# A decayed attention feeding two gated layers on one core: the first pair's sums in two pieces and k's transposes one step earlier

## The chip, the cores and the metric

The kernel runs on one core of one Trainium2 chip. The metric is the device time of one execution, in microseconds (us). The kernel before takes 1025.54 us, the median of three runs (1025.13 to 1026.08). Engines are named as in the profile: PE is TensorE (PEld its weight loads), DVE is VectorE, ACT is ScalarE, POOL is GpSimd, SP is SyncE, which issues the DMAs.

## The reference

Inputs are q, k and v of shape (4, 8, 576, 64), that is 4 batches of 8 heads, and f of shape (4, 8, 576), all in float32. First comes causal attention with a decay, then two layers of products:

```python
scores = (1 / sqrt(64)) * q @ k.T
cum    = cumsum(log(clip(f, 1e-4, 1.0)), axis=-1)
decay  = cum[:, :, :, None] - cum[:, :, None, :]
scores = where(causal, -1e9, scores + decay)
scores = scores - max(scores)
attn   = exp(scores); attn = attn / (sum(attn) + 1e-9)
x      = (attn @ v).transpose(0, 2, 1, 3).reshape(2304, 512)

xn  = x / sqrt(mean(x * x) + 1e-6) * rms_g
g   = xn @ w_gate;  silu = g / (1 + exp(-g))
y   = (silu * (xn @ w_val)) @ w_out          # 512 -> 1536 -> 512
h   = y @ w_in                               # 512 -> 2048
out = (h / (1 + exp(-h))) @ w_out2           # 2048 -> 512
```

## The kernel before, in words

**Attention.** The 32 heads are worked through as 16 pairs, two heads side by side on the 128 partitions. A pair's 576 queries are cut into nine blocks of 64; one block of both heads against its keys is a unit. A unit with block number c has (c+1)*64 keys; the units of a pair run in the order of `ORDER`, that is with 64, 128, 512, 192, 448, 256, 384, 320 and 576 columns. For one unit PE makes the scores in three products (L472: q and k each stand as a high and a low part, and high*high, high*low and low*high are added in one PSUM bank). DVE adds the decay and takes the maximum in one instruction (L475, followed by a short read of the accumulator, tile `nm`). ACT takes the exponential (L488). Four steps later (`TURN`) PE transposes the result in pieces of 128 columns (L497; the 576-column unit has four of these and one more at L504), and DVE or ACT copies them out of PSUM (L278, L280, tiles `g` and `gl`). Six steps later (`USE`) a whole pair is multiplied with v (L528). POOL forms the decay (L459) and the mask on its diagonal (L461) one step ahead of the scores.

**Operands of the next pair.** While a pair runs, k and q of the next are loaded (L396, L398) and transposed by PE (`operand`, L425, tiles `nk` and `nq`, four transposes of 128 columns each; the last 64 rows of both at L442). ACT writes the rounded high part (L273) and DVE the rest (L274), for k as one 128x512 piece each, for q as two halves of 64 partitions. The operands of odd and even pairs lie in the tiles `op0h`, `op0l` and `op1h`, `op1l`. The steps at which this happens are counted from the start of the pair in the table `WHEN`: k at -6, q at -5.

**PSUM.** The scores, and the transposes of k and q, take turns in four banks (tiles called `s`); what is transposed after the exponential, and the first part of the product with v, uses three others (tiles called `t`). A new user of a bank waits until the last reader of the old one is done.

**The start.** `warm` (L247 to L250) multiplies zeros to keep PE busy: 12 products ahead of everything, then 1, 2 and 5 more at three later places (`WARM`). Meanwhile f is clipped (L567, DVE), its logarithm taken (L568, ACT), summed along the row (L570, DVE), scaled (L571, DVE) and negated (L575, ACT); c is transposed (L581) and copied (L584), and for the first pair the negated sums are spread over the partitions by two products with a 0/1 matrix (L411) and copied to `ncb` (L412). The other pairs read them back from DRAM (L419).

**Behind attention.** The weights of the layers are loaded and decoded while attention runs (`weights`, L143 to L154; conversions to high and low parts at L192, L193 and L205, L206). From about 200 us on the kernel consists of PE's products for the layers.

**What sets the order.** The program is written as a loop over steps (L643 on) that runs one unit's part after another, with the rest hung on step numbers by `at` (L630); a scheduler then sorts each engine's instructions, in its own estimate of when they are ready, except where `issue_after` or `later` holds one back. Each engine runs its instructions in that order, one after the other.

Of the kernel before, what the change touches and what calls it, by code (L numbers as in the profile page):

```python
# [30 lines left out]
WARM = (12, 1, 2, 5)  # L31
# [31 lines left out]
def block_kernel(ctx: ExitStack, tc: tile.TileContext, q, k, v, f, w_gate, w_val, w_o1, rms_g, w_in, w_o2, ident_d, sel_d, hot_d, out):  # L63
# [66 lines left out]

    def weights(w, src, cols, key):
# [12 lines left out]
        dst = stp.tile([P, 2 * n], I32, tag="st", name="st")  # L144
        pr = dst.rearrange("p (n t) -> p n t", t=2)
        nc.sync.dma_start(out=dst if cols is None else dst.rearrange("p (c f) -> p c f", f=cols), in_=src)
# [67 lines left out]
    def attention():  # L214
        exps, maxima = [], []
        with ExitStack() as st:
# [30 lines left out]
            def warm(n):  # L247
                ps = bank(pst)
                for _ in range(n):
                    nc.tensor.matmul(ps[:, :384], lhsT=ops[1][0][:, :P], rhs=ops[1][0][:, :384], start=True, stop=True)  # L250
# [21 lines left out]
            def split(hi, lo, src):  # L272
                nc.scalar.activation(out=hi, in_=src, func=AF.Copy)  # L273
                nc.vector.tensor_tensor(out=lo, in0=src, in1=hi.bitcast(F32), op=ALU.subtract)  # L274
# [107 lines left out]
            class Pair:  # L382
# [20 lines left out]
                def load_sums(self, between=None):  # L403
# [4 lines left out]
                    if h == 0:  # L408
                        for w in (slice(0, HS), slice(HS, S)):
                            bp = bank(pss)[:, : w.stop - w.start]  # L410
                            nc.tensor.matmul(bp, lhsT=hot, rhs=n8[:, w], start=True, stop=True)  # L411
                            told = nc.scalar.activation(out=t[:, w], in_=bp, func=AF.Copy)  # L412
                            if w.start == 0:
                                with tc.issue_after(told.ins):
                                    between()
                    else:
                        with tc.issue_after(self.held):
                            for j in range(2):
                                nc.sync.dma_start(out=t[j * D : (j + 1) * D], in_=nc8d[h + j, :].partition_broadcast(D))  # L419

                def operand(self, nm, lone=False):
# [4 lines left out]
                    if nm == "k":  # L426
                        split(self.oh[:, QW + D :], self.ol[:, QW + D :], ps)
                    else:
# [5 lines left out]

                        half(0)
                        if lone:
                            return _p(half, 1)
                        half(1)

                def operand_tails(self):  # L440
                    tl = bank(pss)
                    self.turned = nc.tensor.transpose(tl[:, :P], self.n["q"][:, FULL].rearrange("p j d -> p (j d)"), ident).ins  # L442
                    for j in range(2):
                        js, w = slice(j * D, (j + 1) * D), P - j * D
                        at_ = slice(QW - w, QW + w)
                        hi, lo = (o[js, at_].rearrange("p (i w) -> p i w", w=w)[:, :, :D] for o in (self.oh, self.ol))
                        split(hi, lo, tl[js, :P].rearrange("p (i w) -> p i w", w=D))

            class Rows:
# [13 lines left out]
                def scores(self):  # L463
# [19 lines left out]
                    if c % 2 == 0 and c < BLOCKS - 1:  # L483
                        nc.gpsimd.memset(self.pr[:, n : n + D], 0.0)
# [73 lines left out]
            nc.sync.dma_start(out=hot, in_=hot_d)  # L558
# [18 lines left out]
            with tc.issue_after(pairs[0].turned):  # L577
                warm(WARM[1])
            cps = bank(pss)
            for c in range(BLOCKS):  # L580
                nc.tensor.transpose(cps[:D, c * BH : (c + 1) * BH], c8[:, c * D : (c + 1) * D], ident[:BH, :BH])  # L581
            cj = cps[:D, : BLOCKS * BH].rearrange("p (c n j) -> p c n j", c=BLOCKS, j=2)
            for j in range(2):
                nc.vector.tensor_copy(c8t[j * D : (j + 1) * D], cj[:, :, :, j])  # L584
            second = pairs[0].operand("q", lone=True)
            with tc.issue_after(pairs[0].turned):
                warm(WARM[2])
            pairs[0].load_sums(second)
            pairs[0].operand_tails()
            with tc.issue_after(pairs[0].turned):  # L590
# [446 lines left out]
```

## Time and profile before

| | before |
|---|---|
| median of 3 runs | 1025.54 us (1025.13 to 1026.08) |
| the profiled execution | 1025.31 us |
| its span, first to last instruction | 1023.5 us |
| granted TensorE clock, mean | 1.000 |
| PE busy | 1011.4 us |
| DVE, ACT, POOL busy | 761.1, 566.9, 401.2 us |

The rows further down come from a page that sums up one profiled execution, and from views of its trace. A row of the timeline has the start in us, the duration in us, the engine, the line of the kernel, the operation, its output and inputs with their shapes, and a count; rows that follow each other on one engine with the same line and shape are drawn into one. In square brackets stands how long the engine was idle before it and what ended that. Matmuls are pipelined: the time from one start to the next is what a row of them costs, and the duration shown is longer than that. The same is true to a smaller degree for DVE and ACT: the next instruction often starts 0.05 to 0.1 us before the one ahead ends.

### The profile page before, as it was taken

Reading aid. Unit: us, or ns where it says so; the run is one execution under the profiler, and the core shown is the slowest. Engines: PE = TensorE matmul, PEld = TensorE weight load, DVE = VectorE, ACT = ScalarE, POOL = GpSimd, SP = SyncE. Lnnn points to the kernel's source line nnn. Section 1 sums busy time; section 2 is a strip of 40 time slices with the busy share of each in tenths; the row PEclk is TensorE's granted clock in tenths of the full one; section 3 lists DMA queues with packets and bytes.
Section 4 is the critical chain, followed back from the end, with each engine's and each line's share of the span. In section 5 each row is a group of like instructions: output and inputs, shape, how many; then the busy total and the mean of one; then the engine's idle time right before and its main releaser. Section 6 shows DMA issues by size and latency. Waiting matters only on the chain.

```text
span 1023.5 us, 16104 instructions
## 1 busy us (share of the span) xinstructions
PE 1011.4 (99%) x5463; PEld 847.7 (83%) x5463; DVE 761.1 (74%) x1520; ACT 566.9 (55%) x1193; POOL 401.2 (39%) x613
## 2 busy tenths in 40 slices
PE   9999999999999999999999999999999999999998
PEld 7787788878888888888888888888888888888887
DVE  7889887877778797976688768846666696466664
ACT  7998989873444232544544556564444464534441
POOL 8777666511022026331365334435533322222310
PEclk9999999999999999999999999999999999999999
DMA  5764533123544444231334122223322233121102
GB/s 140 193 189 114 126 92 94 27 63 124 185 142 167 159 150 154 73 124 49 106 124 143 64 65 79 83 83 114 113 83 83 83 124 144 42 71 54 52 1 83
DMA packets 114162, 106.40 MB, mean 104 GB/s; under 512 B 62896, under 2 KB 83792, under 8 KB 114080
## 3 DMA queue, kind: packets, MB, share of 16 engines
q1 hardware_dynamic: 112352, 102.23, 32.5%
q10 hardware_dynamic: 1728, 3.15, 1.0%
q8 instruction: 43, 0.70, 0.3%
q14 instruction: 39, 0.32, 0.1%
HBM read 79.59 MB, written 25.76 MB: 103 GB/s over the span
## 4 chain that ended last, share of the span: by engine, by line
PE 77%; DVE 2%; issue 0%; ACT 0%
PE t L778 40%; PE s L778 20%; PE x L778 16%; PE o L528 0%; DVE hl L696 0%; PE s L303 0%; DVE b11l L696 0%; DVE c L912 0%; PE t L497 0%; PE t L528 0%; DVE f L151 0%; DVE ms L342 0%; ACT pr L488 0%; DVE c L152 0%; DVE wl L174 0%
## 5 line engine op out<-in xcount | busy, mean ns | idle before, releaser
L206 POOL TENSOR_TENSOR wol<-c,woh 128x512 fp32r<-128x512 f32 x53 | 78.7, 1491 | 241.8 <-ACT woh L205 218.3
L696 DVE TENSOR_TENSOR hl<-c,hh 128x512 fp32r<-128x512 f32 (+1 forms) x140 | 114.4, 825 | 45.3 <-ACT hh L695 44.4
L167 POOL TENSOR_TENSOR f<-f 128x256 f32<-128x256 f32 x112 | 93.7, 859 | 112.9 <-DMA f<-keptb 51.2
L695 ACT ACTIVATE hh<-c 128x512 fp32r<-128x512 f32 (+1 forms) x140 | 79.7, 582 | 46.3 <-DVE c L912 41.6
L790 ACT ACTIVATE c<-t 128x512 f32<-128x512 f32 x84 | 49.8, 593 | 95.0 <-PE t L778 93.9
L459 POOL TENSOR_SCALAR dt<-ncb,c8t 128x64 f32<-128x64 f32 (+2 forms) x144 | 79.2, 552 | 35.9 <-DVE nm L475 27.5
L488 ACT ACTIVATE pr<-pr,nm 128x192 f32<-128x192 f32 (+3 forms) x144 | 80.2, 558 | 11.6 <-DVE nm L475 8.1
L905 ACT ACTIVATE c<-c 128x512 f32<-128x512 f32 x66 | 41.6, 630 | 80.8 <-DVE c L795 80.8
L475 DVE CUSTOM_DVE_ANT_0 pr<-s,dt 128x256 f32<-128x256 f32 (+7 forms) x160 | 70.1, 450 | 13.4 <-PE t L497 4.8
L193 POOL TENSOR_TENSOR wl<-f,wh 128x1024 fp32r<-128x1024 f32 x12 | 28.8, 2396 | 125.6 <-ACT wh L192 118.9
L497 PE MATMUL t<-ident,pr 128*128 128x128 f32 x384 | 69.2, 279 | 3.7 <-ACT pr L488 2.6
L174 DVE TENSOR_TENSOR wl<-f,wh 128x1024 fp32r<-128x1024 f32 (+1 forms) x48 | 57.7, 1209 | 20.4 <-ACT wh L172 20.2
L795 DVE TENSOR_TENSOR c<-t,c 128x512 f32<-128x512 f32 x60 | 41.1, 687 | 39.4 <-ACT c L790 26.2
L172 ACT ACTIVATE wh<-f 128x1024 fp32r<-128x1024 f32 (+1 forms) x56 | 54.4, 973 | 23.4 <-PE x L778 18.9
L778 PE MATMUL s<-hh,woh 128*128 128x512 f32 (+1 forms) x172 | 64.0, 372 | 0.2 <-DVE xa L959 0.2
L778 PE MATMUL s<-hh,wol 128*128 128x512 f32 (+1 forms) x172 | 64.0, 372 | 0.0
L778 PE MATMUL s<-hl,woh 128*128 128x512 f32 (+1 forms) x172 | 63.9, 372 | 0.0
L977 DVE TENSOR_TENSOR xa<-x,xa 128x512 f32<-128x512 f32 x64 | 43.5, 682 | 25.2 <-PE x L778 25.1
L977 DVE TENSOR_TENSOR xa<-s,xa 128x512 f32<-128x512 f32 (+1 forms) x63 | 42.9, 683 | 25.5 <-PE s L778 25.1
L905 ACT ACTIVATE c<-t 128x512 f32<-128x512 f32 (+1 forms) x74 | 37.9, 512 | 35.9 <-PE t L778 33.8
L148 ACT ACTIVATE f<-st 128x512 f32<-128x512 f32 x42 | 27.8, 668 | 53.6 <-DMA keptb<-f 18.1
L959 DVE TENSOR_TENSOR xa<-s,xa 128x512 f32<-128x512 f32 (+1 forms) x72 | 45.4, 638 | 14.0 <-PE s L778 13.9
(248 smaller groups left out, 3234.1 us busy)
## 6 DMA issues: line engine op xcount, KB each, us to landing
st<-in_moe_w_out_dram SPq DMA_DIRECT2D x28, 512.0 KB, 3.7
st<-in_moe_w_in_dram SPq DMA_DIRECT2D x16, 512.0 KB, 3.8
f<-keptb SPq DMA_DIRECT2D x32, 256.0 KB, 2.6
st<-in_moe_w_gate_dram SPq DMA_DIRECT2D x12, 512.0 KB, 4.2
kepta<-f SPq DMA_DIRECT2D x24, 256.0 KB, 2.3
st<-in_moe_w_val_dram SPq DMA_DIRECT2D x12, 512.0 KB, 4.6
f<-kepta SPq DMA_DIRECT2D x24, 256.0 KB, 2.8
out_dram<-xa SPq DMA_DIRECT2D x17, 256.0 KB, 2.0
```

The costliest lines, as they stand in the source:

```text
L167: nc.gpsimd.tensor_tensor(out=out_, in0=x, in1=y, op=op)
L174: (nc.gpsimd if plain and i else nc.vector).tensor_tensor(out=lo[i][:, v], in0=f[i][:, v], in1=hi[i][:, v].bitcast(F32), op=ALU.subtract)
L206: nc.gpsimd.tensor_tensor(out=lo, in0=f, in1=hi.bitcast(F32), op=ALU.subtract)
L459: nc.gpsimd.tensor_scalar(out=dt, in0=p.nct[:, 0 if last else D :][:, :n], scalar1=c8t[:, c, p.i : p.i + 1], scalar2=1.0, op0=ALU.add, op1 ...
L475: reduced = nc.vector.tensor_tensor_reduce(out=self.pr[:, ks], in0=sp, in1=self.dt[:, ks], op0=ALU.add, op1=ALU.min, scale=-SCALE, scalar= ...
L488: e = nc.scalar.activation(out=pr, in_=pr, func=AF.Exp, bias=self.nm, scale=-1.0, accum_out=p.batch.sums[:, self.c, p.hp : p.hp + 1])
L497: nc.tensor.transpose(pt[:, jj * P : (jj + 1) * P], keys[:, jj * P : (jj + 1) * P], ident)
L695: nc.scalar.activation(out=hi, in_=src, func=AF.Copy)
L696: nc.vector.tensor_tensor(out=lo, in0=src, in1=hi.bitcast(F32), op=ALU.subtract)
L778: nc.tensor.matmul(ps, lhsT=l, rhs=r, start=start and z == 0, stop=stop and z == len(mms) - 1, skip_group_check=not (start and stop))
L905: act = nc.scalar.activation(out=hf, in_=a, func=AF.Silu)
L977: nc.vector.tensor_tensor(out=a, in0=ps, in1=a, op=ALU.add)
```

## The change

Three things are changed.

- **k's transposes.** From the third pair on (`n > 1`) the step of k in `WHEN` is one smaller, so that PE transposes k of the next pair in front of the four transposes of the 576-column unit (L537 in the new numbering), and no longer behind the scores of the 192-column unit. ACT's and DVE's split of k follows it.
- **The start.** `WARM` goes from (12, 1, 2, 5) to (12, 2, 2, 4). The clip, the logarithm and the sum are each cut in two pieces of 256 and 320 columns. The scaling instruction goes; its factor is put into the two instructions behind (`scale=-ISC` where the sums are negated, a multiplication where c is copied). The negated sums come ahead of k's split on ACT; q is transposed ahead of c; the products that spread the sums come behind the last transpose of q's and k's tails, and both are now issued together.
- **Loads.** The first two loads of w_gate are tied to the load of q of pair 4 (`FETCH`), the 0/1 matrix is loaded ahead of q's tails, and the decay of the first pair's 576-column unit waits for the last clearing of padding on the same engine.

```diff
-WARM = (12, 1, 2, 5)
+WARM = (12, 2, 2, 4)
+HEAD = 256
+FETCH = 4
...
                     for nm in "kq":
-                        at(s + WHEN[nm], _p(p.operand, nm))
+                        at(s + WHEN[nm] - (nm == "k" and n > 1), _p(p.operand, nm))
...
+                        if nm == "q" and not self.i:
+                            nc.sync.dma_start(out=hot, in_=hot_d)
+                        if nm == "q" and self.i == FETCH:
+                            for m in range(2):
+                                fetch_in(w_gate, "a0", m)
...
+                def first_sums(self, w):
+                    if w.start == 0:
+                        self.nct = dec.tile([P, S], F32, tag="ncb", name="ncb", bufs=2)
+                    bp = bank(pss)[:, : w.stop - w.start]
+                    self.spread = nc.tensor.matmul(bp, lhsT=hot, rhs=n8[:, w], start=True, stop=True).ins
+                    def copy():
+                        return nc.scalar.activation(out=self.nct[:, w], in_=bp, func=AF.Copy).ins
+                    return copy
...
-            nc.vector.tensor_scalar(out=lf, in0=ft, scalar1=1e-4, scalar2=1.0, op0=ALU.max, op1=ALU.min)
-            nc.scalar.activation(out=lf, in_=lf, func=AF.Ln)
+            cols = (slice(0, HEAD), slice(HEAD, S))
+            for w in cols:
+                nc.vector.tensor_scalar(out=lf[:, w], in0=ft[:, w], scalar1=1e-4, scalar2=1.0, op0=ALU.max, op1=ALU.min)
+            for w in cols:
+                nc.scalar.activation(out=lf[:, w], in_=lf[:, w], func=AF.Ln)
             table = nc.scalar.activation(out=first, in_=lf[:, :1], func=AF.Exp)
-            nc.vector.tensor_tensor_scan(out=c8, data0=on, data1=lf, initial=0.0, op0=ALU.mult, op1=ALU.add)
-            scaled = nc.vector.tensor_scalar(out=c8, in0=c8, scalar1=ISC, scalar2=None, op0=ALU.mult)
-            with tc.issue_after(table.ins), tc.issue_after(scaled.ins):
-                pairs[0].operand("k")
-            for to, of in ((slice(D, S), slice(0, SF)), (slice(0, D), slice(SF, S))):
-                nc.scalar.activation(out=n8[:, to], in_=c8[:, of], func=AF.Copy, scale=-1.0)
+            for w in cols:
+                before = 0.0 if w.start == 0 else c8[:, HEAD - 1 : HEAD]
+                nc.vector.tensor_tensor_scan(out=c8[:, w], data0=on[:, w], data1=lf[:, w], initial=before, op0=ALU.mult, op1=ALU.add)
+            one = pairs[0]
+            k_parts = one.operand("k", lone=True)
+            with tc.issue_after(one.turned):
+                warmed = warm(WARM[1])
+            with tc.issue_after(warmed):
+                q_parts = one.operand("q", lone=True)
+            with tc.issue_after(table.ins):
+                for to, of in ((slice(D, S), slice(0, SF)), (slice(0, D), slice(SF, S))):
+                    negated = nc.scalar.activation(out=n8[:, to], in_=c8[:, of], func=AF.Copy, scale=-ISC)
...
+            with tc.issue_after(negated.ins):
+                k_high, k_low = k_parts()
...
+            with tc.issue_after(warmed):
+                near, far = (one.first_sums(w) for w in (slice(0, HS), slice(HS, S)))
+            near()
+            far()
+            tails()
+            with tc.issue_after(one.spread):
                 warm(WARM[3])
```

Below is PE's order of before where the sixth pair hands over to the seventh, at 70 to 74 us of the trace; the rows from the 576-column unit's transposes to the scores of the 256-column unit (`op1h` belongs to the pair that runs, `nk` and `nq` are k and q of the next).

```order
L310 MATMUL s<-ident,ss 64x98
L497 MATMUL t<-ident,pr 128x128 x4
L504 MATMUL t<-ident,pr 64x128
L472 MATMUL s<-op1h 128x192
L472 MATMUL s<-op1l,op1h 128x192
L472 MATMUL s<-op1h,op1l 128x192
L425 MATMUL s<-ident,nk 128x128 x4
L497 MATMUL t<-ident,pr 128x128
L472 MATMUL s<-op1h 128x448
```

After the change the same place of PE reads:

```order
L325 MATMUL s<-ident,ss 64x98
L448 MATMUL s<-ident,nk 128x128 x4
L537 MATMUL t<-ident,pr 128x128 x4
L544 MATMUL t<-ident,pr 64x128
L512 MATMUL s<-op1h 128x192
L512 MATMUL s<-op1l,op1h 128x192
L512 MATMUL s<-op1h,op1l 128x192
L537 MATMUL t<-ident,pr 128x128
L512 MATMUL s<-op1h 128x448
```

The four transposes of k went from behind the 192-column scores to ahead of the 576-column unit's transposes; the rest kept its order.

On ACT the same place of before reads as follows (`op0h` 128x512 is k's high part for the next pair, `pr,sums` the exponentials, `wh` a weight's high part):

```order
L488 ACTIVATE pr,sums<-pr,nm 128x128
L192 ACTIVATE wh<-f 128x1024
L488 ACTIVATE pr,sums<-pr,nm 128x512
L278 ACTIVATE gl_145<-t 64x128
L488 ACTIVATE pr,sums<-pr,nm 128x192
L273 ACTIVATE op0h<-s 128x512
```

and after the change:

```order
L528 ACTIVATE pr,sums<-pr,nm 128x128
L205 ACTIVATE wh<-f 128x1024
L528 ACTIVATE pr,sums<-pr,nm 128x512
L287 ACTIVATE op0h<-s 128x512
L293 ACTIVATE gl_145<-t 64x128
L528 ACTIVATE pr,sums<-pr,nm 128x192
```

k's high part moved ahead of two instructions, and still stands behind the weight's conversion and the exponential of 512 columns.

On DVE, again at this place, before (`g` 128x4x128 is the copy of the 576-column unit's transposes, the instructions called ISA are those with the maximum, now L515):

```order
L280 COPY g_1225<-t 128x4x128
L475 ISA pr,nm<-s,dt 128x192
L475 ISA nm 128x1
L280 COPY g_1398<-t 128x128
L475 ISA pr,nm<-s,dt 128x448
L475 ISA nm 128x1
L274 TENSOR_TENSOR op0l<-s,op0h 128x512
```

and after the change:

```order
L295 COPY g_1231<-t 128x4x128
L288 TENSOR_TENSOR op0l<-s,op0h 128x512
L515 ISA pr,nm<-s,dt 128x192
L515 ISA nm 128x1
L295 COPY g_1404<-t 128x128
L515 ISA pr,nm<-s,dt 128x448
L515 ISA nm 128x1
```

k's low part moved from behind the 448-column unit to ahead of the 192-column unit.

## Rows read from the trace of the kernel before

**Rows 1.** The page: busy time, share of the span and instructions of each engine.

```profile
PE 1011.4 (99%) x5463; PEld 847.7 (83%) x5463; DVE 761.1 (74%) x1520; ACT 566.9 (55%) x1193; POOL 401.2 (39%) x613
```

**Rows 2.** Stretches: from:to, us, then busy us of each engine, PEclk, DMA share, GB/s.

```profile
12.00:187.00 175.00, 169.05 (x1347) 141.08 (x1345) 146.17 (x532) 160.69 (x472) 124.29 (x324) 1.00 0.52 134
...
200.00:1000.00 800.00, 798.86 (x3870) 670.15 (x3870) 582.95 (x905) 382.67 (x666) 259.60 (x240) 1.00 0.30 99
```

**Rows 3.** Waits of PE: tile and line, what ended them: us, times, longest.

```profile
PE t L497 <- ACT pr L488: 2.6, 8, 0.5
...
PE s L371 <- DVE nm L475: 1.0, 1, 1.0
```

**Rows 4.** Timeline at 110 to 113 us, PE and DVE.

```profile
110.03 0.66 PE L497 MATMUL t<-ident,pr 128*128 128x128 f32 x4 [0.45 <-ACT pr L488]
...
111.27 0.69 DVE L280 COPY g<-t 128x512 f32<-128x512 f32 x1
...
111.87 0.35 DVE L475 CUSTOM_DVE_ANT_0 pr<-s,dt 128x192 f32<-128x192 f32 x1
...
112.57 0.36 PE L472 MATMUL s<-op0h 128*128 128x256 f32 x1
```

**Rows 5.** Timeline at 71 to 75 us, PE.

```profile
71.31 0.60 PE L425 MATMUL s<-ident,nk 128*128 128x128 f32 x4
...
71.75 0.27 PE L497 MATMUL t<-ident,pr 128*128 128x128 f32 x1
...
72.46 0.60 PE L425 MATMUL s<-ident,nq 128*128 128x128 f32 x4
...
73.77 0.39 PE L472 MATMUL s<-op1h 128*128 128x256 f32 x1
```

**Rows 6.** Timeline at 71 to 75 us, ACT and DVE.

```profile
71.22 1.05 ACT L192 ACTIVATE wh<-f 128x1024 fp32r<-128x1024 f32 x1
...
72.17 0.72 ACT L488 ACTIVATE pr<-pr,nm 128x512 f32<-128x512 f32 x1
...
72.88 0.26 ACT L278 ACTIVATE gl<-t 64x128 f32<-64x128 f32 x1
...
74.09 0.69 DVE L274 TENSOR_TENSOR op0l<-s,op0h 128x512 fp32r<-128x512 f32 x1 [0.67 <-ACT op0h L273]
```

**Rows 7.** Timeline of ACT at 112, 118, 124 and 175 us.

```profile
112.77 0.58 ACT L273 ACTIVATE op1h<-s 128x512 fp32r<-128x512 f32 x1
...
118.53 0.63 ACT L205 ACTIVATE woh<-f 128x512 fp32r<-128x512 f32 x1
...
124.36 0.73 ACT L488 ACTIVATE pr<-pr,nm 128x512 f32<-128x512 f32 x1
...
174.89 0.72 ACT L488 ACTIVATE pr<-pr,nm 128x512 f32<-128x512 f32 x1
```

**Rows 8.** Timeline of PE at 126 and 177 us.

```profile
126.03 0.65 PE L528 MATMUL t<-g,vn 128*64 128x256 f32 x2
126.61 0.39 PE L472 MATMUL s<-op1h 128*128 128x256 f32 x1
...
177.46 0.39 PE L472 MATMUL s<-op1h 128*128 128x256 f32 x1
```

**Rows 9.** Timeline at 151 to 153 us, DVE and PE.

```profile
151.80 0.35 DVE L475 CUSTOM_DVE_ANT_0 pr<-s,dt 128x192 f32<-128x192 f32 x1
...
152.21 0.39 PE L472 MATMUL s<-op1h 128*128 128x256 f32 x1
```

**Rows 10.** Timeline of the start.

```profile
1.32 4.21 PE L250 MATMUL t<-op1h 128*128 128x384 f32 x12 [1.32 <-DVE op1h L245]
...
6.26 0.46 DVE L571 TENSOR_SCALAR c<-c 32x576 f32<-32x576 f32 x1
...
6.89 0.76 ACT L575 ACTIVATE n<-c 32x512 f32<-32x512 f32 x2
...
9.37 1.12 PE L250 MATMUL t<-op1h 128*128 128x384 f32 x5
```

More of the change, by code (lines that the diff above doesn't have):

```diff
@@ L129, in words, with fetch, fetch_in @@
         return (w, 1) if w.dtype == F32 else (w.bitcast(I32), 2)
+    fetched = {}
+    def fetch(src, cols):
+        dst = stp.tile([P, 2 * DM], I32, tag="st", name="st")
+        nc.sync.dma_start(out=dst if cols is None else dst.rearrange("p (c f) -> p c f", f=cols), in_=src)
+        return dst
+    def fetch_in(w, key, m):
+        w, s = words(w)
+        if s > 1:
+            fetched[key, m] = fetch(w[:, s * m * P : s * (m + 1) * P].rearrange("(c p) f -> p c f", p=P), s * P)
     def weights(w, src, cols, key):
@@ L214, in attention @@
     def attention():
-        exps, maxima = [], []
+        exps, maxima, padded = [], [], []
         with ExitStack() as st:
@@ L272, in split @@
             def split(hi, lo, src):
-                nc.scalar.activation(out=hi, in_=src, func=AF.Copy)
-                nc.vector.tensor_tensor(out=lo, in0=src, in1=hi.bitcast(F32), op=ALU.subtract)
+                high = nc.scalar.activation(out=hi, in_=src, func=AF.Copy)
+                low = nc.vector.tensor_tensor(out=lo, in0=src, in1=hi.bitcast(F32), op=ALU.subtract)
+                return high, low
             def move(which, out, in_):
@@ L407, in load_sums @@
                     h = b * H + 2 * hp
[L408 to L419, printed above, removed]
+                    with tc.issue_after(self.held):
+                        for j in range(2):
+                            nc.sync.dma_start(out=t[j * D : (j + 1) * D], in_=nc8d[h + j, :].partition_broadcast(D))
                 def operand(self, nm, lone=False):
@@ L426, in operand @@
                     if nm == "k":
-                        split(self.oh[:, QW + D :], self.ol[:, QW + D :], ps)
+                        whole = _p(split, self.oh[:, QW + D :], self.ol[:, QW + D :], ps)
+                        if lone:
+                            return whole
+                        whole()
                     else:
@@ L433, in half, with halves, operand_tails, both @@
                             split(hi, lo, ps[js].rearrange("p (c w) -> p c w", w=D))
+                        def halves():
+                            parts = [[o[j * D : (j + 1) * D, : FULL * 2 * P].rearrange("p (c j w) -> p c j w", j=2, w=D)[:, :, j] for o in (self.oh, self.ol)] for j in range(2)]
+                            of = [ps[j * D : (j + 1) * D].rearrange("p (c w) -> p c w", w=D) for j in range(2)]
+                            for (hi, lo), src in zip(parts, of):
+                                nc.scalar.activation(out=hi, in_=src, func=AF.Copy)
+                            for (hi, lo), src in zip(parts, of):
+                                nc.vector.tensor_tensor(out=lo, in0=src, in1=hi.bitcast(F32), op=ALU.subtract)
+                        if lone:
+                            return halves
                         half(0)
-                        if lone:
-                            return _p(half, 1)
                         half(1)
-                def operand_tails(self):
+                def operand_tails(self, lone=False):
                     tl = bank(pss)
                     self.turned = nc.tensor.transpose(tl[:, :P], self.n["q"][:, FULL].rearrange("p j d -> p (j d)"), ident).ins
[L443 to L447, printed above, removed]
+                    def both():
+                        for j in range(2):
+                            js, w = slice(j * D, (j + 1) * D), P - j * D
+                            at_ = slice(QW - w, QW + w)
+                            hi, lo = (o[js, at_].rearrange("p (i w) -> p i w", w=w)[:, :, :D] for o in (self.oh, self.ol))
+                            split(hi, lo, tl[js, :P].rearrange("p (i w) -> p i w", w=D))
+                    if lone:
+                        return both
+                    both()
             class Rows:
@@ L576, in attention @@
+            with tc.issue_after(table.ins):
+                for to, of in ((slice(D, S), slice(0, SF)), (slice(0, D), slice(SF, S))):
+                    negated = nc.scalar.activation(out=n8[:, to], in_=c8[:, of], func=AF.Copy, scale=-ISC)
             nc.sync.dma_start(out=nc8d, in_=n8)
[L577 to L578 removed]
+            with tc.issue_after(negated.ins):
+                k_high, k_low = k_parts()
             cps = bank(pss)
[L580 to L581 removed]
+            with tc.issue_after(one.turned):
+                for c in range(BLOCKS):
+                    turned = nc.tensor.transpose(cps[:D, c * BH : (c + 1) * BH], c8[:, c * D : (c + 1) * D], ident[:BH, :BH])
@@ L582, in attention @@
             cj = cps[:D, : BLOCKS * BH].rearrange("p (c n j) -> p c n j", c=BLOCKS, j=2)
[L583 to L590, printed above, removed]
+            with tc.issue_after(k_low.ins):
+                for j in range(2):
+                    scaled = nc.vector.tensor_scalar(out=c8t[j * D : (j + 1) * D], in0=cj[:, :, :, j], scalar1=ISC, scalar2=None, op0=ALU.mult)
@@ new lines, in attention @@
+            with tc.issue_after(k_high.ins), tc.issue_after(scaled.ins):
+                q_parts()
+            with tc.issue_after(turned.ins):
+                tails = one.operand_tails(lone=True)
+            with tc.issue_after(one.turned):
+                warmed = warm(WARM[2])
+            with tc.issue_after(warmed):
[4 more added lines that the diff above has]
+            with tc.issue_after(one.spread):
```

14 lines of the change are left out of this document (7 added, 7 removed).

## The prediction

> **What bounds the kernel now.** I read the busy times first: PE is at work for 1011.4 of 1023.5 us, the next engine, DVE, for 761.1 [rows 1]. Then the stretches. From 200 to 1000 us PE is busy for 798.86 of 800 us, so nothing can be won there, and what attention gives up or wins before goes straight to the end. In attention, 12 to 187 us, PE is busy for 169.05 of 175 us, ACT for 160.69, DVE for 146.17 [rows 2]. So PE has some 6 us of idle time there, and ACT, at 92%, has hardly more than twice that: whatever is put ahead of an exponential on ACT pushes work that PE waits for. Third the waits of PE: the largest group is the one in front of the 576-column unit's transposes, which wait for ACT's exponential, 2.6 us in eight waits of at most 0.5 us; the longest single wait is 1.0 us, at the sums of squares [rows 3]. Seven of the eight stand where one pair hands over to the next. Last I followed the hand-overs in the timeline one by one, and set beside each the order that the changed program has there and what each instruction there waits for.
>
> **k's transposes moved.** Fourteen hand-overs are changed, at 22, 33, 45, 57, 71, 84, 98, 110, 124, 137, 149, 162, 175 and 188 us. PE's four transposes of k take 0.44 us from their start to the next instruction's [rows 5]. Put ahead of the 576-column transposes, they fill the wait, which is at most 0.45 us (110.03 in [rows 4]). But the transposes lie in one of four banks, and the bank is handed on only when DVE has made k's low part. By the bank order of the changed program the bank's next user is, at most hand-overs, the 256-column unit with its scores, and at three of them the transposes of q. What counts is when k's split is done.
>
> - At 22, 33 and 45 us the split is done before its bank is wanted. The waits that go there are 0 at 22 us, 0.14 and 0.16 us at the others: -0.30.
> - At 57, 110 and 162 us the 0.45 us wait goes, but the 256-column scores now wait for k's low part, which stands behind the copy of 512 columns. At 110: that copy starts at 111.27 and the next instruction 0.60 later, at 111.87 [rows 4]; the split takes 0.68 to 112.55, and the scores start some 0.06 later at 112.61, against 112.57 before [rows 4]. So +0.04 each, +0.12 together: the gain is eaten up.
> - At 84, 137 and 188 us the 256-column scores waited for the maximum of the 192-column unit and still do: 0.
> - At 98 and 149 us there was no wait to be won, and k's split now stands between the copy and the maximum of the 192-column unit. At 149 the copy is done at 151.80, when the 192-column maximum started [rows 9]; the split ends 0.69 later [rows 6], at 152.49, and the scores start at 152.55 against 152.21 [rows 9]: +0.34. At 98 worked in the same way +0.32. Together +0.66.
> - At 71, 124 and 175 us an earlier tile of the sums of squares shifts the turn of the banks, and it is q's transposes that take k's bank. PE then stands still from the end of the 448-column scores until k is split, and the split is late, since its high part on ACT stands behind the exponential of 512 columns, which is itself behind a weight's conversion. At 71: the exponential starts at 72.17 and what follows it at 72.88 [rows 6]; k's high part takes 0.58 [rows 7] to 73.46, the low part 0.71 with its start (0.69 in [rows 6]) to 74.17, q's transposes start near 74.20 (72.46 before) and take 0.44, so that the 256-column scores start at 74.64 and not at 73.77 [rows 5]: +0.87. At 124 the conversion of a weight that stood at 118.53 [rows 7] moves behind and in front of this exponential: 0.55 us (its 0.63 less the overlap). So 124.36 [rows 7] becomes 124.91; 0.71, 0.58 and 0.71 more are 126.91, and with 0.06 and 0.44 the scores start at 127.41 against 126.61 [rows 8]: +0.80; one of the two products with v that stood ahead of them now stands behind, at 0.29 (126.03 to 126.61 for two [rows 8]): +1.09. At 175 the exponential is earlier against PE: 174.89 [rows 7] and the same 2.00 are 176.89, the scores start at 177.39 against 177.46 [rows 8], -0.07, and with the 0.29 it is +0.22. Together +2.18.
>
> Behind these points PE's later work hangs on the same banks and on DVE's maxima, which move along, so I let the delays stand in full.
>
> **The start.** The scaling of 0.46 us [rows 10] goes from the path, and cutting clip, logarithm and sum in two allows some overlap. Against this, the negated sums (two instructions, 0.76 [rows 10]) now stand ahead of k's high part on ACT and no longer behind it, and the product that spreads the first piece of the sums gets the bank of k's transposes: it waits for k's low part now, which only the second piece did before. The bounds are the whole scaling won (-0.46) and the whole of the negation lost (+0.76). I take their sum, +0.30, since both lie on the one path from the sums to the spread; what the overlap of pieces gives is taken back by POOL, whose decays follow each other without a gap behind it. The warming products stay 20 in number.
>
> **The loads.** w_gate's first two loads were issued between the loads of k and q of pair 4 and are now behind q's, some 4 us later; they feed a conversion on DVE and ACT that nothing in attention waits for. Zero; if the cover fails, it costs POOL or ACT time inside the waits already counted.
>
> **The sum.** -0.30 + 0.12 + 0 + 0.66 + 2.18 + 0.30 = +2.96 us. The profiled execution took 1025.31 us, 0.23 under the median, so it stands for the others; on the median this gives 1028.5 us. What the unknown terms allow: the start from -0.46 to +0.76, and the waits at 71, 124 and 175 from 0.5 (if the conversions on ACT come a place later) to 3.0 (if the delay of the 192- and 448-column maxima behind the split also holds up the exponentials and the transposes after them): 1026.1 to 1029.8.
>
> **The clock.** In this trace the granted clock is 1.00 in every stretch from 12 us on, though PE waits up to 1.0 us at a time [rows 2, 3]. The new waits at 71 and 124 us are about 1.6 us long. The Trainium skill, on the page "TensorE: Matmul & The Clock Gate", has TensorE lose its full clock when it idles; by that rule PE could fall to half speed behind such a wait. By this trace the 1.0 us wait did not do it, so it is a rival and no term.
>
> **Rivals.**
>
> 1. The move does what it says: the waits in front of the 576-column transposes are filled and nothing takes their place, because k's split comes earlier than I have it. Then 0.16, 0.14, three of 0.45 (0.44 filled) and three of some 0.32 go, 2.6 us in all [rows 3], and with the start at -0.46 the time is 1025.54 - 3.0 = 1022.5. For it: the group of waits is there and k's transposes fit in. Against it: ACT's high part of k has to be finished, and at seven of the fourteen hand-overs it is queued behind the exponential of 512 columns. It decides where ACT's split ends before PE has done the 448-column scores. Chance 0.13.
> 2. The new waits are made good: PE waits later anyway, 1.0 us at the sums of squares [rows 3] and, of the 6 us that it is idle in attention [rows 2], some in smaller pieces (I estimate 1.3 of use) up to its end, and what is late by then costs nothing. Of 2.96 some 2.3 are taken back: 1026.2, within what counts as no change. Against it: most of these waits are for DVE or ACT, and both are held up by the same split. Chance 0.30.
> 3. The clock falls behind the three waits. Twelve warming products of the start took 4.21 us, 0.35 each, five later ones 1.12, 0.22 each [rows 10]; those stand at the lower and the higher of the two levels, 1.2 and 2.4 GHz, with idle time ahead of the first and work ahead of the others. A stretch as long as the first at the lower level loses 4.21 - 12 * 0.22 = 1.6 us, three of them 4.7: 1033.2. Chance 0.04.
>
> **How the numbers follow.** My forecast, k's split late and three new waits of PE, has a chance of 0.53 and lies at 1026.1 to 1029.8. A measurement of this kernel can tell 0.2%, 2.05 us, from no change: below 1023.5 is faster, above 1027.6 slower. The forecast is above this in about nine cases of ten (0.49), inside in the rest (0.04); of rival 1 0.12 is faster, and rival 2 counts as same. Rival 3 adds 0.04 to slower. That is slower 0.53, same 0.35, faster 0.12. The range from 1023.8 to 1030.2 takes in rival 2, the bounds of the start and of the waits, and leaves out most of rivals 1 and 3.
>
> **What would show it.** In the trace of the changed kernel: the group of waits in front of the 576-column transposes, 2.6 us now, is nearly gone; in its place stand waits of q's transposes for DVE's low part of k, over 1 us each at 71 and 124 us, and short ones of the 256-column scores at the other hand-overs; the crossing of 71 us starts within 0.5 us of where it was and the one of 137 us is later by some 2 us. The first scores of 512 columns at the start come later by a few tenths. I would be wrong if q's transposes wait for nothing, if ACT makes k's high part ahead of the exponential of 512 columns at 71 and 124, or if the hand-over at 188 us stands no later than it did.

## The result, and the profile after

The changed kernel takes 1031.18 us, the median of six runs (1030.12 to 1032.30), beside 1025.28 us for the kernel before: 1.0053 times as long, with a 95% interval of 1.0043 to 1.0064, so slower by 4.4 to 6.6 us. The forecast had the direction, but its 1028.5 us and its range up to 1030.2 were too low. The profiled execution is the fastest of the six, 1030.12 us, 4.81 over that of before; three of the six lie near 1030.3 and three near 1032.1, and what makes these two groups is not explained here.

The page's busy times, one stretch of attention and the same late stretch as before; the columns are those of [rows 1, 2]:

```profile
PE 1011.9 (98%) x5463; PEld 845.4 (82%) x5463; DVE 759.0 (74%) x1521; ACT 566.6 (55%) x1194; POOL 403.1 (39%) x613
```

```profile
12.00:192.00 180.00, 170.39 (x1350) 140.14 (x1349) 145.89 (x531) 160.96 (x474) 126.53 (x327) 1.00 0.51 130
200.00:1000.00 800.00, 798.43 (x3882) 670.02 (x3881) 584.05 (x920) 385.03 (x678) 262.77 (x247) 1.00 0.31 99
```

No engine works longer: PE's busy time grows by 0.5 us, and the span by 4.8. What grew is PE's idle time in attention, from 6.0 us of 175 to 9.6 of 180. From 200 us on nothing changed. The waits of PE (total, times, longest), to set beside [rows 3]:

```profile
PE t L537 <- ACT pr L528: 1.6, 5, 0.4
PE s L386 <- DVE op1l L288: 1.4, 1, 1.4
...
PE s L448 <- issue: 1.2, 1, 1.2
PE s L512 <- DVE nm L515: 1.2, 3, 0.7
...
PE t L568 <- ACT gl L293: 0.8, 1, 0.8
PE s L448 <- PE s L512: 0.6, 1, 0.6
```

The eight waits of 2.6 us for an exponential are down to five of 1.6, and none of these five is in front of a 576-column unit any more. In their place stand waits of q's transposes (L448, at 130 and 181 us), one of a product with v (L568, at 75 us) and three for a maximum (L512).

Where they fall is read from two marks in each pair: the start of the 384-column scores, behind the hand-over, and the start of the 512-column scores of the next pair, behind the pair's end. The table gives by how much each stretch between two marks grew against the kernel before, in us. The last column belongs to experiments told below; it compares two kernels that decode no weights before 72 us.

| stretch | predicted | k's step alone | changed kernel | k's step, decoding later |
|---|---|---|---|---|
| start, to 15.8 us | +0.30 | +0.14 | 0.00 | -0.11 |
| hand-overs at 22, 33, 45 | -0.30 | -0.23, -0.10, +0.09 | -0.23, -0.09, -0.63 | -0.26, -0.11, -0.10 |
| 57 | +0.04 | +0.24 | -0.26 | +0.06 |
| 71 | +0.87 | +1.15 | +1.15 | +0.04 |
| 84, 137, 188 | 0 | 0.00, -0.05, -0.02 | 0.00, -0.03, -0.02 | +0.18, +0.01, -0.01 |
| 98, 149 | +0.32, +0.34 | +0.32, +0.32 | +0.32, +0.32 | +0.33, +0.33 |
| 110, 162 | +0.04, +0.04 | +0.05, +0.08 | +0.06, +0.08 | -0.44, +0.45 |
| 124 | +1.09 | +0.65 | +0.65 | +0.94 |
| 175 | +0.22 | +0.04 | +0.04 | +0.10 |
| all hand-overs | +2.66 | +2.54 | +1.36 | +1.52 |
| pair's end at 39, 52, 64 | not counted | +0.78, +0.67, +0.47 | +1.28, +0.90, +0.47 | 0.00, 0.00, 0.00 |
| other pair's ends | not counted | +0.32 | +0.61 | +0.16 |
| in all, to 206.5 us | +2.96 | +4.92 | +4.62 | +1.57 |

With k's step alone the hand-overs sum to nearly what was worked out, 2.54 against 2.66. In the changed kernel they sum to only 1.36, since those at 45 and 57 us give back 0.89 of what the pairs' ends ahead of them lost. What the sum lacked are the ends of the pairs at 39 to 69 us.

### The profile page after: what moved, and what is told of

The parts are those of the page before. It is cut to its first block, busy times and chain, and to the rows that moved or that the text cites. A ratio compares the mean times of both kernels' runs of the same rounds, so it can differ in the third digit from the quotient of the medians.

```text
span 1028.3 us, 16120 instructions
## 1 busy us (share of the span) xinstructions
PE 1011.9 (98%) x5463; PEld 845.4 (82%) x5463; DVE 759.0 (74%) x1521; ACT 566.6 (55%) x1194; POOL 403.1 (39%) x613
## 4 chain that ended last, share of the span: by engine, by line
PE 77%; DVE 2%; DMA 0%; issue 0%; ACT 0%; SPq 0%; ACTq 0%
PE t L835 39%; PE s L835 20%; PE x L835 16%; DMA st<-in_moe_w_in_dram 0%; PE o L568 0%; PE s L318 0%; DVE b11l L753 0%; DVE hl L753 0%; PE t L537 0%; PE t L568 0%; DVE c L969 0%; DVE ms L357 0%; ACT pr L528 0%; DVE c L165 0%; DVE wl L187 0%
## 5 line engine op out<-in xcount | busy, mean ns | idle before, releaser
L515 DVE CUSTOM_DVE_ANT_0 pr<-s,dt 128x256 f32<-128x256 f32 (+7 forms) x160 | 70.2, 449 | 12.4 <-PE t L537 5.2
L537 PE MATMUL t<-ident,pr 128*128 128x128 f32 x384 | 68.6, 279 | 3.1 <-ACT pr L528 1.6
```

The source lines that it names most:

```text
L515: reduced = nc.vector.tensor_tensor_reduce(out=self.pr[:, ks], in0=sp, in1=self.dt[:, ks], op0=ALU.add, op1=ALU.min, scale=-SCALE, scalar= ...
L537: nc.tensor.transpose(pt[:, jj * P : (jj + 1) * P], keys[:, jj * P : (jj + 1) * P], ident)
```

## Experiments

Each kernel was timed in five rounds beside the kernel before.

**1. The parts alone.** k's step on the kernel before:

```diff
-                        at(s + WHEN[nm], _p(p.operand, nm))
+                        at(s + WHEN[nm] - (nm == "k" and n > 1), _p(p.operand, nm))
```

> The kernel before with k's transposes one step earlier and nothing else. Theory A, two causes (k's split late at the hand-overs, and apart from it the loads of w_gate that come later in the changed kernel and hold ACT up at 39 us): about 3.5 us over before, 1028.8, and the hand-over at 45 us no later than before. Theory B, all of it comes from k's step: 5 to 6 us over before, with the hand-over at 45 us a us late. Theory C, the start and its loads do it: within 1 us of before.

The changed kernel without k's step (the line above, undone in it):

> The changed kernel with k's transposes at their old step: start and loads alone. Theory A: about 1.2 us over before, 1026.5, all of it gone by 45 us. Theory B: as before, 1025 to 1025.6. Theory C: 4 to 6 us over before.

The same without the tied loads as well:

```diff
-                        if nm == "q" and self.i == FETCH:
-                            for m in range(2):
-                                fetch_in(w_gate, "a0", m)
```

> As the one above, but without tying w_gate's first two loads to q of pair 4, so that the second of them comes behind the load of the next pair's k. Theory A: 1 to 2 us over before, ACT or DVE waiting for a load near 40 us. Theory B: as before. Theory C: 4 to 6 us over before.

The changed kernel without the tied loads (the same diff), with k's step:

> The changed kernel with k's step and start, but without tying w_gate's first two loads to q of pair 4: the loads come last of all versions, behind the sums and the next pair's k. Theory A: at least as slow as the changed kernel, 1031 to 1033, if it is the lateness of these loads that holds up ACT at 39 us; faster, near 1029, if it is their collision with q's load. Theory B: as the changed kernel, 1031. Theory C: slower than the changed kernel by 1 us or more.

Measured: k's step alone 1030.11 us, ratio 1.0041 (1.0029 to 1.0054) with 1025.84 for before; start and loads 1026.81, 1.0010 (1.0001 to 1.0018); the start without the tied loads 1027.41, 1.0015 (1.0006 to 1.0023); the changed kernel without them 1031.45, 1.0052 (1.0039 to 1.0066). So most of the loss comes with k's step, about 4.3 us of it, and the start costs 1.0 us with its tied loads and 1.6 without them. Theory A was right on the start and had k's step too small: the hand-over at 45 us was late with k's step alone too (its 192-column scores start 0.61 us later), with w_gate loaded no later. The tied loads help by 0.6 us or less.

In k's step alone the pair's end at 39 us reads as follows, ACT, DVE and PE (the two marks are the rows with 384 and with 512 columns):

```profile
37.61 0.37 ACT L278 ACTIVATE xa<-t 128x256 f32<-128x256 f32 x1
38.00 0.59 ACT L273 ACTIVATE op1h<-s 64x512 fp32r<-64x512 f32 x1
38.62 1.25 ACT L148 ACTIVATE f<-st 128x512 f32<-128x512 f32 x2
...
38.63 0.69 DVE L274 TENSOR_TENSOR op1l<-s,op1h 64x512 fp32r<-64x512 f32 x1 [1.31 <-ACT op1h L273]
39.35 0.97 DVE L149 TENSOR_SCALAR f<-f 128x512 f32<-128x512 f32 x2
...
41.50 0.54 DVE L475 CUSTOM_DVE_ANT_0 pr<-s,dt 128x384 f32<-128x384 f32 x1
...
42.08 0.29 DVE L274 TENSOR_TENSOR op1l<-s,op1h 64x128 fp32r<-64x128 f32 x1
...
39.22 0.42 PE L472 MATMUL s<-op0h 128*128 128x384 f32 x1
...
42.10 0.39 PE L472 MATMUL s<-op0h 128*128 128x256 f32 x1 [0.58 <-DVE nm L475]
...
44.41 0.48 PE L472 MATMUL s<-op1h 128*128 128x512 f32 x1
```

and in the kernel before:

```profile
36.96 0.69 ACT L148 ACTIVATE f<-st 128x512 f32<-128x512 f32 x1
37.68 0.59 ACT L273 ACTIVATE op1h<-s 64x512 fp32r<-64x512 f32 x1
...
37.68 0.43 DVE L149 TENSOR_SCALAR f<-f 128x512 f32<-128x512 f32 x1
...
41.17 0.29 DVE L274 TENSOR_TENSOR op1l<-s,op1h 64x128 fp32r<-64x128 f32 x1
41.49 0.56 DVE L475 CUSTOM_DVE_ANT_0 pr<-s,dt 128x384 f32<-128x384 f32 x1
...
39.44 0.42 PE L472 MATMUL s<-op0h 128*128 128x384 f32 x1
...
41.61 0.35 PE L472 MATMUL s<-op0h 128*128 128x256 f32 x1
...
43.85 0.48 PE L472 MATMUL s<-op1h 128*128 128x512 f32 x1
```

L148 and L149 are the first two steps of decoding a weight. Before, one decoding step stood on ACT at 36.96, ahead of q's second half, and DVE began on it at 37.68. With k's step the order on ACT has both decoding steps behind q's second half, which itself moved behind an exponential and a copy; DVE is idle for 1.31 us, decodes later, and the tails of q and k come 0.9 us later. PE's second piece of the 576-column scores (128x256), which stood without a wait before, waits 0.58 us for the maximum of the 384-column unit. That maximum stands on DVE behind the decoding steps, and now ahead of the last tail. Before, the second piece started while the same maximum was still running, so it had another bank; how much of the loss is the bank and how much DVE's order was not told apart.

The pair's end at 64 us loses its 0.47 us in the same way: the second piece waits 0.68 us for the same maximum, where before it waited 0.24 us for the last tail. The one at 52 us does not. There the second piece has no wait, and it is a weight's conversion that moved, from a hand-over to the pair's end, first before and then with k's step alone:

```profile
47.65 1.06 ACT L192 ACTIVATE wh<-f 128x1024 fp32r<-128x1024 f32 x1
```

```profile
51.94 1.06 ACT L192 ACTIVATE wh<-f 128x1024 fp32r<-128x1024 f32 x1
```

All that is behind it on ACT comes later, and the three groups of PE's transposes at 55.17, 55.76 and 56.79 us start 0.58 us late together, the last of them after a wait of 0.20 us for an exponential.

**2. Where k's step costs.** Three edits of k's step, and one of the loads in the changed kernel without k's step:

```diff
# at 71, 124 and 175 us only
-                        at(s + WHEN[nm] - (nm == "k" and n > 1), _p(p.operand, nm))
+                        at(s + WHEN[nm] - (nm == "k" and n in (6, 10, 14)), _p(p.operand, nm))
```

> The kernel before with k's transposes one step earlier at three hand-overs alone, those of 71, 124 and 175 us, where q's transposes take k's bank. The prediction's term for these: +2.2 us, 1027.7. Rival, read from the hand-over times of the changed kernel (71 to 84 us +0.69, 124 to 137 +0.20, 175 to 188 -0.39): about +0.5, 1026.

```diff
# from 84 us on
-                        at(s + WHEN[nm] - (nm == "k" and n > 1), _p(p.operand, nm))
+                        at(s + WHEN[nm] - (nm == "k" and n > 6), _p(p.operand, nm))
```

> The kernel before with k's step earlier only from the hand-over of 84 us on. If the cost of k's step lies in the first five hand-overs, where weights are decoded beside attention: +1.5 to 2, 1027.3. If it is spread evenly over all: +2.9, 1028.7. If it sits at 71, 124 and 175, as the prediction has it: +2.1, with a wait over 1 us at 124.

```diff
# everywhere, with a higher rank for the split
+HI = 60
...
-                        split(self.oh[:, QW + D :], self.ol[:, QW + D :], ps)
+                        with tc.high_priority(offset=HI) if self.i > 1 else ExitStack():
+                            split(self.oh[:, QW + D :], self.ol[:, QW + D :], ps)
...
-                        at(s + WHEN[nm], _p(p.operand, nm))
+                        at(s + WHEN[nm] - (nm == "k" and n > 1), _p(p.operand, nm))
```

> The kernel before with k's step earlier at all hand-overs, and k's split given a higher rank in the scheduler, so that ACT makes the high part ahead of the exponential of 512 columns at 22, 71, 84 and 137 us (still behind it at 124). If the split's place on ACT is what costs (the prediction's reason): about 1 us faster than k's step alone, 1029, the wait at 71 us gone or under 0.3 us. If not (bank order at the end of each pair, or DVE's order): as k's step alone, 1030, or slower, since the exponential is later.

```diff
# no k's step; w_gate's first loads ahead of q's
-                        if nm == "q" and self.i == FETCH:
+                        if nm == "k" and self.i == FETCH:
```

> The changed kernel without k's step, and with w_gate's first two loads ahead of q's load of pair 4, where the kernel before has them. If it is these loads that cost: at most 0.3 us over before, 1025.5 to 1025.9, and the waits at 42 to 48 us gone. If the reordered start costs by itself: as without this edit, 1026.8.

Measured: 1026.85 us, 1.0015 (1.0006 to 1.0024), for the three hand-overs; 1027.20, 1.0017 (1.0008 to 1.0026), from 84 us on; 1030.33, 1.0045 (1.0033 to 1.0058), with the rank; 1026.73, 1.0012 (1.0003 to 1.0021), with the early loads. The kernel before had 1025.39.

The three hand-overs alone cost 1.5 us, between the prediction's 2.2 and its rival's 0.5. By the two marks the one at 71 us costs 0.88 there, as forecast (0.87); the 1.15 of the table comes only where the hand-overs ahead of it are moved too. The wait of q's transposes for k's low part is there as forecast, at 71 us:

```profile
74.32 0.66 PE L425 MATMUL s<-ident,nq 128*128 128x128 f32 x4 [1.52 <-DVE op0l L274]
```

From 84 us on the cost is 1.8 us, so the larger part lies in the first five hand-overs and the pairs' ends between them. The rank did what it was to do and won nothing: ACT makes k's high part first, and now the exponential of 512 columns is late instead.

```profile
74.02 1.06 ACT L193 ACTIVATE wh<-f 128x1024 fp32r<-128x1024 f32 x1
74.99 0.58 ACT L274 ACTIVATE op0h<-s 128x512 fp32r<-128x512 f32 x1
75.46 0.71 ACT L490 ACTIVATE pr<-pr,nm 128x512 f32<-128x512 f32 x1
```

```profile
76.39 0.63 PE L426 MATMUL s<-ident,nq 128*128 128x128 f32 x4 [0.87 <-PE s L474]
```

The hand-over at 71 us cost 0.57 instead of 1.15 there, but those at 84, 137 and 188 us, free before, cost 0.31 to 0.35 each, and the one at 22 us cost 0.24 where it had won 0.23. And the loads' place is not the whole of the start's cost: with it undone the time stayed.

**3. Without decoding.** The decoding of the first weights is released by an exponential with the number `PLACE`. Put three pairs later, it leaves the pairs' ends up to 69 us, and no weight conversion stands at 71 us. The control, with k's step, and with the start alone:

```diff
-PLACE = 22
+PLACE = 49
```

> The kernel before with the decoding of the layers' first weights put three pairs later (it starts behind the exponential number 49 and no longer number 22). Control for the next two: within 1 us of before, with the waits at 42 to 48 and 66 us gone or moved.

> The one above with k's transposes one step earlier at all hand-overs. If the decoding beside attention is what makes the pair ends late once k is moved: the stretches from the 384-column scores to the next pair's 512-column scores at 39, 52 and 64 us cost under 0.1 us each against the one above (0.78, 0.67 and 0.47 with decoding), and the hand-over at 71 us, with no weight conversion ahead of the exponential, costs 0.3 and not 1.15: in all 1.5 to 2.5 us over the one above. If the bank order alone does it: 4 us or more over the one above.

> The reordered start alone (neither k's step nor the tied loads) with the same later decoding. If the start costs only through the decoding at 39 to 56 us: within 0.3 us of the control, and the stretch at 39 us adds under 0.1. If the new order of the start costs by itself: 0.8 us or more over the control.

> The kernel before with k's step earlier at the hand-over of 22 us alone, which was ahead by 0.23 us with k's step everywhere. Faster by 0.2 us in the trace from 28 us on, 1025.1, which the times can hardly tell from before; if the 0.23 is given back at the end of the pair or by the decoding at 39 us, the same as before or slower by 0.5.

(the last is the kernel before with `n == 2` in the line of k's step.)

Measured: 1027.48, 1029.39, 1027.85 and 1025.23 us, with 1025.38 for before; ratios 1.0019 (1.0010 to 1.0028), 1.0037 (1.0024 to 1.0050), 1.0024 (1.0015 to 1.0033) and 0.9995 (0.9986 to 1.0004). The control itself lost 2.1 us, where I had allowed 1; what counts below is the distance from it, and that settles where the missing part comes from. With decoding out of the way k's step costs exactly nothing at the ends of the pairs at 39, 52 and 64 us, and 0.04 at the hand-over of 71 (table, last column); it is ahead of its control by 0.57 us at 55 us. In all it still costs 1.9 us over its control, 1.57 of it in the table, nearly all at hand-overs. Behind 72 us, where the decoding now is, the pairs' ends move by -0.46 to +0.43 us and sum to +0.16: decoding beside k's step does not cost the same everywhere. The start alone stands within 0.01 us of its control at every mark from 16 us on, so in attention it costs only through the decoding; its median is 0.37 us above the control's all the same, and the median time from first to last instruction is 1025.7 us in both, so that this rest lies outside what the trace shows. The hand-over at 71 without the conversion, ACT and PE:

```profile
69.33 0.72 ACT L488 ACTIVATE pr<-pr,nm 128x512 f32<-128x512 f32 x1
...
70.06 0.57 ACT L273 ACTIVATE op0h<-s 128x512 fp32r<-128x512 f32 x1
```

```profile
71.45 0.63 PE L425 MATMUL s<-ident,nq 128*128 128x128 f32 x4 [0.62 <-PE s L472]
...
71.95 0.36 PE L472 MATMUL s<-op1h 128*128 128x256 f32 x1
```

The exponential starts 0.2 us before the pair's last transposes (69.54) and not 1.1 us behind them, and k's split is in time for all but 0.62 us, which the filled gap and the moved products with v pay for.

**4. The order of decoding.** k's step with `PLACE = 20`; the changed kernel with early loads (the diff of `FETCH` above); and k's step at 22, 33 and 45 us alone with `PLACE = 20`:

> The kernel before with k's step earlier at all hand-overs, and the decoding of the first weights released two exponentials earlier (behind number 20, not 22), so that its first step on ACT stands ahead of the 192- and the 448-column exponentials of the pair at 33 to 44 us and no longer behind the last half of q. If the decoding made late by the new order on ACT is what costs at the end of that pair: the stretch at 39 us costs under 0.3 us over before (0.78 with k's step alone), and the total falls by 0.5 to 1.5 us to 1028.6 to 1029.6. If the changed bank order alone costs there: 0.7 us or more remain. If the load is not there in time, ACT waits and it is slower than 1030.1.

> The changed kernel with w_gate's first two loads ahead of q's load of pair 4. If the late load (ACT waited 0.87 us for it at 39.3 us) is the start's share of the cost: the stretch at 39 us costs 0.8 and not 1.28 us, and the total is that of k's step alone, 1030.1, or less. If not: as the changed kernel, 1031.

> k's step earlier only at 22, 33 and 45 us, where the split is done in time, with the decoding released at number 20. The hand-overs gain 0.3 to 0.5 us and, if the decoding is not late, nothing is given back: 1024.9 to 1025.2 against 1025.4, which the times can hardly tell apart. If the decoding still ends late: 1025.5 to 1026.5.

Measured: 1028.73 us, 1.0033 (1.0021 to 1.0045); 1030.83, 1.0054 (1.0042 to 1.0067); 1028.57, 1.0033 (1.0020 to 1.0046); before 1025.35. Released earlier, the pair's end at 39 us still costs 0.88 us, and not under 0.3 as I had expected. But the hand-over behind it, at 45 us, now takes 0.63 us less than before, so that the two stretches cost 0.25 us together, against 0.87 with k's step alone. ACT reaches the decoding before the load has landed, and in order as it works, all behind it waits:

```profile
35.97 0.68 ACT L148 ACTIVATE f<-st 128x512 f32<-128x512 f32 x1 [0.36 <-DMA st<-in_moe_w_gate_dram]
```

In the third kernel that wait is 1.99 us, and the 0.3 us won at the hand-overs of 22 and 33 us is lost eightfold at this pair's end. The total of the first falls by 1.4 us; by the marks this is won at the hand-over of 45 us, at the pair's end at 52 us (+0.17 and no longer +0.67; the conversion stands at 48.21 us, at the hand-over again) and at the hand-overs of 71 and 124 us (+0.68, +0.15). The early loads take the stretch at 39 us from 1.28 back to 0.78, as expected of the wait that the changed kernel has there,

```profile
39.32 0.67 ACT L161 ACTIVATE f<-st 128x512 f32<-128x512 f32 x1 [0.87 <-DMA st<-in_moe_w_gate_dram]
```

but the 0.63 us that the changed kernel got back at 45 us is gone too, and the time stays.

No version beat the kernel before: k's step at 22 us alone cannot be told from it.

## Why the prediction was right in direction and wrong in size

**The hand-overs**, with k's step alone, were right in most places: -0.24 for the first three against -0.30, +0.32 and +0.32 at 98 and 149, near zero at 84, 137 and 188, +0.05 and +0.08 at 110 and 162. That the sum agrees to 0.12 us is luck in part: 57 and 71 were too small (0.24 and 1.15 for 0.04 and 0.87), 124 and 175 too large (0.65 and 0.04 for 1.09 and 0.22), and these errors cancel. At 124 and 175 the 0.29 us for a product with v that moves behind q's transposes was too much: at 124 in the changed kernel the first two of these products stand behind, and from the 256-column to the 384-column scores it is 3.91 us, against 3.92 before. In the changed kernel the hand-overs sum to 1.36, half the forecast. The reason given for 71 holds: in the changed kernel, ACT, DVE and PE,

```profile
72.89 1.06 ACT L205 ACTIVATE wh<-f 128x1024 fp32r<-128x1024 f32 x1
73.86 0.71 ACT L528 ACTIVATE pr<-pr,nm 128x512 f32<-128x512 f32 x1
...
74.56 0.58 ACT L287 ACTIVATE op0h<-s 128x512 fp32r<-128x512 f32 x1
75.04 0.26 ACT L293 ACTIVATE gl<-t 64x128 f32<-64x128 f32 x1
```

```profile
75.17 0.69 DVE L288 TENSOR_TENSOR op0l<-s,op0h 128x512 fp32r<-128x512 f32 x1 [1.10 <-ACT op0h L287]
```

```profile
75.35 0.65 PE L568 MATMUL t<-g,vn 128*64 128x256 f32 x2 [0.83 <-ACT gl L293]
75.93 0.66 PE L448 MATMUL s<-ident,nq 128*128 128x128 f32 x4
76.34 0.36 PE L512 MATMUL s<-op1h 128*128 128x256 f32 x1
```

k's high part stands behind the conversion and the exponential, as in [rows 6] with the numbers moved by 1.7 us, the low part waits 1.10 us for it, and q's transposes start when it is done. One thing was not foreseen: the copy `gl` stands behind k's high part too, and the product with v, queued ahead of q's transposes on PE, waits for that.

**The step that failed** is the one behind the hand-overs: "Behind these points PE's later work hangs on the same banks and on DVE's maxima, which move along, so I let the delays stand in full", and beside it, for the loads, "Zero". Both took the rest of a pair as unchanged. It was not: where weights are decoded, at 39 to 69 us, the earlier k changed the scheduler's order of q's halves, copies, decoding steps and conversions on ACT and DVE. At 39 and 64 us the second piece of the 576-column scores then waited for DVE, at 52 us transposes came late behind ACT. That is 1.92 of the 4.92 us with k's step alone, and zero without decoding; in the changed kernel it is 2.65 of 4.62, of which the hand-overs at 45 and 57 us give back 0.89. The zero for the loads rested on the reason that nothing in attention waits for them. They were issued 2.2 us later than before, not 4, and still ACT stood still for 0.87 us at 39 us, waiting for the first of them, with exponentials behind it. I had compared the two orders at the hand-overs only. ACT's busy share of 92% in [rows 2] was read, and used for the hand-overs alone.

**The start** was too high by 0.3 us by itself: 0.00 at 15.8 us. Its first 512-column scores did not come some tenths later, as forecast, but 0.33 us earlier (10.86 for 11.19), and the 384-column scores at 15.77 in both kernels. Its cost came 25 us later, by the same road: a later load and a later order of decoding, 0.8 us in that stretch without k's step, and 0.5 with the loads put back as well. In the traces the two meet in the same stretch and do not add up (4.92 and 0.83 alone, 4.62 together); by the medians they do (4.3 and 1.0 alone, 5.9 together).

**Rivals.** The waits filled with nothing in their place: the first three hand-overs did that, for 0.24 us with k's step alone. Delays made good by later waits: the wait that the prediction puts at the sums of squares, 1.0 us in [rows 3] (the transposes of the factors made from them), did not shrink but grew to 1.4. The clock did not fall: behind the longest new wait, 1.52 us, it was granted in full (the kernel with three hand-overs alone, columns as in [rows 2]).

```profile
72.00:74.40 2.40, 0.88 (x6) 0.53 (x6) 1.11 (x3) 1.70 (x5) 2.32 (x4) 1.00 0.97 243
74.40:78.00 3.60, 3.60 (x35) 2.53 (x35) 2.37 (x10) 3.04 (x9) 3.43 (x9) 1.00 0.62 180
```

The granted clock alone is weak evidence, since it reads 1.00 also at 1.30 to 5.50 us of the kernel before, where the products take 0.35 us and later ones 0.22 [rows 10]. But the products with v behind this wait are as quick as those with no such wait ahead, in the kernel with three hand-overs and with k's step alone:

```profile
75.97 2.11 PE L528 MATMUL o<-g,vn 128*64 128x320 f32 x16
```

```profile
36.55 2.11 PE L528 MATMUL o<-g,vn 128*64 128x320 f32 x16
```

The rule that the prediction weighed, from the Trainium skill ("TensorE: Matmul & The Clock Gate", the part on the clock gate), is that TensorE runs at its lower clock when it has been idle. No wait in attention shows it at work here.

**Open** are the two groups of times of the changed kernel: the account above is of its fastest execution, 4.8 us over before, and the 1.1 us by which the median lies above that are not located. The kernel whose trace has the longest wait for a load spreads most (1027.12 to 1031.53 us, against 1030.07 to 1030.71 with k's step alone), but that loads landing at different times make the groups is a guess that no run here tries. Open too is which single instruction on ACT or DVE decides the end of a pair under decoding: releasing the decoding earlier changed too much at once.

## What to carry to other kernels

A move that fills a wait of one engine is paid for where the other engines are full: follow the new order on each of them through the whole period of the loop, not only round the place of the move, and look hardest where rare work (here the decoding of weights) shares an engine at over 90%. To tell the parts apart, take that rare work away and make the move again: a cost that goes to zero then belongs to both together. Comparing the starts of two marks per period between two traces shows where time went, mostly to 0.1 us: stretches that no edit touched mostly agree within 0.05 us, but those up to 21 us differ by up to 0.3.

## What the runs showed of the hardware that was not expected

An engine that works in order passes a load's lateness on to all that is queued behind: decoding released two exponentials earlier met a load that was not there, and ACT stood still for 0.36 us in one kernel and for 1.99 us in another that differed from it in k's step alone. Why the load landed so differently was not tried.
